# Weight conversion moved through a PSUM bank and spread over four head pairs of an attention stage; the last pair's running sums moved to VectorE

## The chip, the cores and the metric

The kernel runs on one core of one Trainium2 chip. The metric is the device time of one execution in microseconds, median of several runs. One execution of each kernel was also recorded by the hardware profiler, and all rows below come from that record.

## The reference

Three stages follow each other. Attention has 2 batches, 8 heads, 1152 keys and a head size of 64; neighbouring query rows are averaged, so that 576 queries remain for each head. Two MLPs (512 to 2048 to 512) then run over the 1152 tokens.

```python
q_pool = q.reshape(B, H, S // 2, 2, D).mean(axis=3)
scores = (1 / sqrt(D)) * q_pool @ k^T
attn = exp(scores - max(scores)) ; attn = attn / (sum(attn) + 1e-9)
x = (attn @ v) rearranged to [1152 tokens, 512]
x = leaky_relu(x @ moe_w_in, 0.01) @ moe_w_out
out = silu(x @ moe2_w_in) @ moe2_w_out
```

Query and key are scaled up in the inputs, so that the maximum has to be subtracted. Query, key and value are float32. The MLP weights are float64: the kernel sees each as a pair of 32-bit words and makes a float32 number of it (the "conversion" below), and each number is then split into a high part that TensorE reads directly and a low part.

## The kernel before

Attention takes the heads two at a time: eight pairs, p = 0 to 7. A pair has nine key tiles t and two heads j. These are its steps, with their lines:

- Transposes of queries and keys on TensorE (line 431), each held in a PSUM bank until ScalarE (line 348) and VectorE (lines 488, 527) have read it. These are done for the next pair while the present one runs.
- Maxima: 27 score tiles of the next pair are computed (lines 576 to 580) and each is reduced by VectorE straight out of its bank (line 584, tile `mx`). The row of maxima goes by small DMAs into the operand `ql` (line 602 onwards).
- Scores (line 634, tile `pss`), exponentials on ScalarE (line 638, tile `e`), and the product with the values (line 666, tile `pv`).
- Running sums over the key tiles, `acc += e` (line 655): 16 additions for a pair, t = 1 to 8 for each j. They run on GpSimd; in the last pair, seven of the 16 run on VectorE (`dve_last`).
- After a pair: the sums over the partitions (line 694, tile `psum`), a reciprocal that goes out and back by four DMAs with one VectorE instruction between them (line 729, tile `cmp`), and `finish` (lines 763 to 767): multiply, high part on ScalarE, low part on VectorE. The last pair has `sums_last` instead (lines 740 to 754), without DMAs.

The conversion of one piece of weights (128x512) has five steps in `convert_steps`: `begin` on ScalarE (line 127), then `clamp`, `shift`, `sign` and `tail` on VectorE (lines 131, 135, 139, 145). `clamp` and `shift` work in place on the tile `wt` in SBUF; `sign` and `tail` read one of the raw words (`wraw`, SBUF) and `wt`, and write `wt`. Eight pieces are converted during attention and 56 later, between the matmuls of the MLPs. Four of the eight are also split during attention (line 163 on ScalarE, line 167 on GpSimd).

The order of the instructions on each engine is made when the program is built, by a list scheduler (`Plan`). Every task has an engine, an assumed duration, a due time, and tokens that it takes and gives back. A task becomes ready when what it needs is done in the planner's own clock; among the ready tasks whose tokens are free, the one with the earliest due time comes next. The planner's clock gives a pair `t` = 30 us and the first begins at `t0` = 18 us. Its durations are guesses: they fix the order, and the engines then run it in order, each waiting where it must. Six PSUM banks (`bank`) are shared by transposes, maxima, scores and sums. TensorE runs in order too, and the first MLP's matmuls (line 923, tile `ph`) come behind the last pair's sums; the MLPs reuse attention's PSUM banks. A weight load takes one of three `raw` buffers, a conversion one of four `wt` buffers.

Of the kernel before, what the change touches and what calls it, by code (L numbers as in the profile page):

```python
# [8 lines left out]
F32 = mybir.dt.float32  # L9
F32R = mybir.dt.float32r  # L10
ACTF = mybir.ActivationFunctionType
ALU = mybir.AluOpType
U32 = mybir.dt.uint32
# [6 lines left out]
def pooled_attention_two_mlps(  # L20
# [28 lines left out]
    t=30.0,  # L49
# [5 lines left out]
    sums=1.15,  # L55
    norm=1.55,
    dve_add=(),
    dve_last=((3, 0), (4, 1), (5, 0), (6, 1), (7, 0), (8, 0), (8, 1)),
    low_pool=((0, 0, 1), (0, 1, 0), (0, 1, 1)),
    ql_pool=(0, 1),  # L60
    lead=3,
    load0=8.0,
    load1=12.0,
    weights=(-3.0, -0.3),
    conv=8,
    split=4,
    wt=4,
# [5 lines left out]
class Weights:  # L73
# [40 lines left out]
        for step in self.convert_steps():  # L114
            step()

    def convert_steps(self):
        nc = self.nc
        box = {}

        def begin():
            pairs = self.raw.pop(self.n_convert).rearrange("p (f w) -> p f w", w=2)
            box["low"], box["high"] = pairs[:, :, 0], pairs[:, :, 1]
            box["t"] = t = self.wt_p.tile(list(box["high"].shape), U32, tag="wt", name="wt")
            box["tf"] = self.mid[self.n_convert] = t.bitcast(F32)
            self.n_convert += 1
            nc.scalar.activation(out=box["tf"], in_=box["high"].bitcast(F32), func=ACTF.Abs, scale=65536.0)  # L127

        def clamp():
            tf = box["tf"]  # L130
            nc.vector.tensor_scalar(out=tf, in0=tf, scalar1=2.0, scalar2=W_TOP, op0=ALU.max, op1=ALU.min)  # L131

        def shift():
            t = box["t"]
            nc.vector.tensor_scalar(out=t, in0=t, scalar1=4, scalar2=1, op0=ALU.logical_shift_left, op1=ALU.logical_shift_right)  # L135

        def sign():
            t = box["t"]
            nc.vector.scalar_tensor_tensor(  # L139
                out=t, in0=box["high"], scalar=0x80000000, in1=t, op0=ALU.bitwise_and, op1=ALU.bitwise_or  # L140
            )

        def tail():
            t = box["t"]
            nc.vector.scalar_tensor_tensor(  # L145
                out=t, in0=box["low"], scalar=29, in1=t, op0=ALU.logical_shift_right, op1=ALU.bitwise_or
            )

        return begin, clamp, shift, sign, tail
# [35 lines left out]
class Plan:  # L185
# [15 lines left out]
    def add(self, engine, weight, due, emit=None, after=(), order=(), take=(), give=(), lag=None, begin=0.0):  # L201
        t = dict(
            engine=engine, weight=weight, due=due, emit=emit, take=take, give=give, left=0, at=begin, next=[],
            lag=self.LAG[engine] if lag is None else lag, n=len(self.tasks),
        )
        self.tasks.append(t)
        for x in after:
            self.edge(x, t)
        for x in order:
            self.edge(x, t, 0.0)  # L210
        return t
# [72 lines left out]
def attention(ctx, tc, q, k, v, xh, xl, weights):  # L284
# [8 lines left out]
    NP = B * H // 2  # L293
# [7 lines left out]
    P = PARAMS  # L301
    T0, T = P["t0"], P["t"]
# [11 lines left out]
    add = plan.add  # L314
    plan.tokens(bank=NBANK, qnat=1, knat=2, vnat=2, q2=1, ops=3, acc=2, pvs=1, v=1, r=1, raw=3, wt=P["wt"])
    plan.ring("e", NE)
    banks = list(range(NBANK))

    def bank(name):
        i = banks.pop(0)  # L320
        return ps_b.tile([128, 512], F32, tag=f"b{i}", name=name), i
# [16 lines left out]
    knat, qnat, vnat, q2, K2, QH, mx, acc, e_t, vps, pvs, rec, box = ({} for _ in range(13))  # L338
# [309 lines left out]
    def sum_up(p, t, j, after, order, due):  # L648
        on_dve = (p, t, j) in dve_adds

        def go():
            e = nc.vector if on_dve else nc.gpsimd
            if t == 1:
                acc[p, j] = sm_p.tile([128, SQ], F32, tag="acc", name="acc", bufs=4)
            e.tensor_tensor(out=acc[p, j], in0=e_t[p, j, 0] if t == 1 else acc[p, j], in1=e_t[p, j, t], op=ALU.add)  # L655

        take = ("acc",) if t == 1 and j == 0 else ()
        return add("DVE" if on_dve else "POOL", 1.2 if on_dve else 1.45, due, go, after=after, order=order, take=take)

    def pv(p, t, due, after, order):  # L660
        def go():
# [96 lines left out]
    def finish(p, after, due):  # L758
        b, hp = divmod(p, HP)
        cs = slice(b * SQ, (b + 1) * SQ)  # L760
        flat = lambda: pvs[p].rearrange("p a c -> p (a c)")
        x = add(
            "DVE", 0.95, due, lambda: nc.vector.tensor_tensor(out=pvs[p], in0=pvs[p], in1=rec.pop(p), op=ALU.mult),
            after=after, give=("r",),
        )
        x = add("ACT", 0.69, due, lambda: nc.scalar.activation(out=xh[:, hp, cs], in_=flat(), func=ACTF.Copy), after=[x])
        low = lambda: nc.vector.tensor_tensor(out=xl[:, hp, cs], in0=flat(), in1=xh[:, hp, cs], op=ALU.subtract)
        return add("DVE", 0.8, due + 1.0, low, after=[x], give=("pvs",))
# [24 lines left out]
    for p in range(NP):  # L793
        at = lambda x: T0 + (p + x) * T
        out = {}
        due = 0.0 if p == 0 else P["load1"] if p == 1 else at(P["load"])
# [23 lines left out]
        for n in range(NM):  # L820
            lo, hi = P["max"]
            due = 1.0 + 0.55 * n if p == 0 else at(lo + (hi - lo) * n / NM)
            j, u = n // NA, n % NA // NCH
            maxima.setdefault((j, u), []).append(max_tile(p, n, out, due))
        for j in range(2):
            after = scored.get((p - 3, j), []) + (filled[p] if p < 3 else [])
# [4 lines left out]
        steps = [(t, j) for t in range(NKT) for j in range(2)]  # L831
        if p == 0:
            steps = [(t, 0) for t in range(P["lead"])]
            for t in range(NKT):
                steps += [(t, 1)] + [(t + P["lead"], 0)] * (t + P["lead"] < NKT)
        for i, (t, j) in enumerate(steps):
            due = at(i / (2 * NKT))
# [5 lines left out]
        last = []  # L843
# [8 lines left out]
        values = evac_pv(p, last[0], at(1.0) + 1.0)  # L852
        ends = [av[NKT - 1, 0], av[NKT - 1, 1]]
        if p < NP - 1:
            finish(p, sums(p, ends, at(P["sums"])) + values, at(P["norm"]))
        else:
            finish(p, sums_last(p, ends, at(1.0)) + values, at(1.0))

    def weight_steps():
        convs, order = [], []
        n = P["conv"] + 3
        for i in range(n):
            lo, hi = P["weights"]
            begin = T0 + (NP + lo + (hi - lo) * i / n) * T
            due = T0 + (NP - 0.9 + 0.9 * i / n) * T
            x = add("SP", 0.5, due, weights.load, order=order, take=("raw",), lag=5.0, begin=begin)
            order = [x]
            if i >= P["conv"]:  # L870
                continue
            weigh = (("ACT", 0.66), ("DVE", 0.8), ("DVE", 1.0), ("DVE", 0.8), ("DVE", 0.8))
            for m, (step, (eng, w)) in enumerate(zip(weights.convert_steps(), weigh)):
                x = add(
                    eng, w, due, step, after=[x], order=convs[-1:] if m == 0 else [],
                    take=("wt",) if m == 0 else (), give=("raw",) if m == 4 else (),
                )
            convs.append(x)
        last = []
        for i in range(P["split"]):  # L880
            due = T0 + (NP - 1 + i / P["split"]) * T
            high, low = weights.split_steps()
            x = add("ACT", 0.62, due, high, after=[convs[i]], order=last)
            last = [add("POOL", 1.45, due, low, after=[x], give=("wt",))]

    weight_steps()
    plan.run()
# [186 lines left out]
```

## Time and profile before

| | |
|---|---|
| median of three runs (lowest, highest) | 687.91 us (686.66, 688.94) |
| the profiled execution | 688.05 us, its span 686.3 us |
| TensorE busy | 657.7 us, 96% of the span |
| VectorE, ScalarE, GpSimd busy | 466.6, 321.7, 398.9 us |
| mean granted TensorE clock | 0.985 of full speed |
| first matmul of the MLPs | at 274.32 us of the span |

The span runs from the first to the last instruction, and the execution's own time is 1.75 us longer. A stretch named below by its ends in microseconds counts from the start of the span. Engines are named in the rows as PE (TensorE), DVE (VectorE), ACT (ScalarE), POOL (GpSimd) and SP (SyncE, whose queue issues all DMAs). An instruction of one group may begin a little before the one ahead of it has ended, so sums of durations can be slightly above the busy time.

### The profile page before, as it was taken

The numbers are of one execution on the slowest core, as the hardware profiler recorded it, in microseconds if no ns is written. First come the engines' busy times: TensorE is split into PE (matmuls) and PEld (weight loads), VectorE is DVE, ScalarE is ACT, GpSimd is POOL, SyncE is SP. The second block draws the span as 40 slices with busy tenths as digits, with TensorE's granted clock in tenths as the row PEclk, the third lists the DMA queues.
The fourth block names the chain that finished last, engine by engine and source line by source line (L and its number), as shares of the span: only waits on it lengthen the run. The fifth ranks groups of instructions, "written<-read, shape, count | busy, mean of one in ns | idle before, by whom it ended". The sixth has DMA issues, their size and how long they took to land.

```text
span 686.3 us, 10321 instructions
## 1 busy us (share of the span) xinstructions
PE 657.7 (96%) x3741; PEld 533.7 (78%) x3741; DVE 466.6 (68%) x689; ACT 321.7 (47%) x694; POOL 398.9 (58%) x303
## 2 busy tenths in 40 slices
PE   6899999999979988999999999999989999999997
PEld 4566776767756754898988989999878898898986
DVE  6775758577789979497667567367666578877222
ACT  5446667575737555464533334244434543334120
POOL 7476888878868984565454354364634444455220
PEclk9899999999999999999999999999989999999999
DMA  5535151534634123032322223113122322220012
GB/s 147 154 79 140 36 139 37 156 80 125 182 84 120 49 63 105 5 124 93 123 92 78 77 94 91 62 60 95 61 77 78 92 93 69 88 89 1 0 47 92
DMA packets 41898, 59.71 MB, mean 87 GB/s; under 512 B 15324, under 2 KB 24568, under 8 KB 41848
## 3 DMA queue, kind: packets, MB, share of 16 engines
q1 hardware_dynamic: 41848, 59.07, 29.6%
q8 instruction: 29, 0.48, 0.3%
q14 instruction: 21, 0.17, 0.1%
HBM read 49.81 MB, written 2.42 MB: 76 GB/s over the span
## 4 chain that ended last, share of the span: by engine, by line
PE 76%; DVE 13%; issue 4%; ACT 4%; DMA 2%; SPq 1%; ACTq 0%; DVEq 0%
PE ph L923 25%; PE po L957 13%; PE pf L985 12%; PE pss L634 9%; PE pv L666 9%; PE pmx L580 4%; DVE mx L584 3%; PE prep L431 2%; DVE wt L135 2%; DVE wt L139 2%; DVE wt L131 2%; DVE a L942 1%; ACT wt L127 1%; DVE ql L488 1%; DVE wt L145 1%
## 5 line engine op out<-in xcount | busy, mean ns | idle before, releaser
L944 POOL TENSOR_TENSOR gl<-a,gh 128x512 fp32r<-128x512 f32 (+1 forms) x64 | 95.1, 1488 | 163.4 <-ACT gh L943 107.5
L655 POOL TENSOR_TENSOR acc<-acc,e 128x576 f32<-128x576 f32 x105 | 154.7, 1494 | 33.2 <-ACT e L638 27.4
L638 ACT ACTIVATE e<-pss 128x288 f32<-128x288 f32 x288 | 101.8, 411 | 84.9 <-PE pss L634 80.7
L584 DVE TENSOR_REDUCE mx<-pmx 128x1 f32<-128x384 f32 x216 | 110.5, 550 | 33.7 <-PE pmx L580 29.1
L923 PE MATMUL ph<-xh,w0h 128*128 128x320 f32 (+1 forms) x384 | 109.7, 340 | 4.2 <-DVE a L942 3.6
L923 PE MATMUL ph<-xl,w0h 128*128 128x320 f32 (+1 forms) x384 | 109.3, 339 | 0.0
L923 PE MATMUL ph<-xh,w0l 128*128 128x320 f32 (+1 forms) x384 | 109.0, 338 | 0.0
L131 DVE TENSOR_SCALAR wt<-wt 128x512 f32<-128x512 f32 x64 | 51.0, 797 | 81.4 <-ACT wt L127 72.6
L634 PE MATMUL pss<-qh,k 128*128 128x288 f32 x288 | 87.8, 321 | 2.2 <-DVE mx L584 2.0
L666 PE MATMUL pv<-e,vnat 128*64 128x288 f32 x576 | 87.7, 425 | 1.2 <-ACT e L638 1.2
L634 PE MATMUL pss<-ql,ka 128*128 128x288 f32 x288 | 82.2, 301 | 4.3 <-DMA ql<-mn 4.3
L923 PEld LDWEIGHTS ph<-xh,w0h 128*128 128x128 f32 x384 | 68.4, 191 | 12.0 <-DVE a L942 4.7
L923 PEld LDWEIGHTS ph<-xh,w0l 128*128 128x128 f32 x384 | 67.7, 190 | 5.0
L923 PEld LDWEIGHTS ph<-xl,w0h 128*128 128x128 f32 x384 | 67.9, 191 | 4.7
L634 PEld LDWEIGHTS pss<-qh,k 128*128 128x128 f32 x288 | 55.4, 192 | 20.2 <-issue 8.3
L580 PE MATMUL pmx<-k,qh 128*128 128x384 f32 x192 | 66.0, 383 | 4.9 <-DVE mx L584 3.0
L943 ACT ACTIVATE gh<-a 128x512 fp32r<-128x512 f32 (+1 forms) x32 | 22.0, 687 | 95.1 <-DVE a L942 95.1
L145 DVE SCALAR_TENSOR_TENSOR wt<-wraw,wt 128x512 uint32<-128x512 uint32 x64 | 62.6, 978 | 2.0
L135 DVE TENSOR_SCALAR wt<-wt 128x512 uint32<-128x512 uint32 x64 | 62.0, 970 | 2.1
L139 DVE SCALAR_TENSOR_TENSOR wt<-wraw,wt 128x512 uint32<-128x512 uint32 x64 | 58.7, 917 | 2.0
L666 PEld LDWEIGHTS pv<-e,vnat 128*64 128x64 f32 x576 | 35.6, 138 | 31.3 <-issue 14.3
L634 PEld LDWEIGHTS pss<-ql,ka 128*128 128x128 f32 x288 | 55.6, 193 | 5.0 <-DMA ql<-mn 3.0
(76 smaller groups left out, 1126.5 us busy)
## 6 DMA issues: line engine op xcount, KB each, us to landing
wraw<-in_moe_w_in_dram SPq DMA_DIRECT2D x32, 512.0 KB, 3.8
wraw<-in_moe_w_out_dram SPq DMA_DIRECT2D x32, 512.0 KB, 3.3
vnat<-in_v_dram SPq DMA_DIRECT2D x8, 576.0 KB, 4.8
qnat<-in_q_dram SPq DMA_DIRECT2D x16, 256.0 KB, 6.2
knat<-in_k_dram SPq DMA_DIRECT2D x7, 576.0 KB, 4.2
ka<-k SPq DMA_DIRECT2D x16, 160.0 KB, 2.6
out_dram<-acc SPq DMA_DIRECT2D x9, 256.0 KB, 2.0
ka<-k SPq DMA_DIRECT2D x16, 128.0 KB, 2.6
```

The source lines that it names most:

```text
L135: nc.vector.tensor_scalar(out=t, in0=t, scalar1=4, scalar2=1, op0=ALU.logical_shift_left, op1=ALU.logical_shift_right)
L139: nc.vector.scalar_tensor_tensor(out=t, in0=box["high"], scalar=0x80000000, in1=t, op0=ALU.bitwise_and, op1=ALU.bitwise_or)
L580: nc.tensor.matmul(out=ps[:, 0:KC], lhsT=QH[p, j][:, t * 128:(t + 1) * 128], rhs=K2[p, j][:, ks], start=True, stop=True)
L584: nc.vector.tensor_reduce(out=mx[p][:, n:n + 1], in_=ps[:, 0:KC], op=ALU.max, axis=AX.X)
L634: nc.tensor.matmul(out=ps[:, 0:C], lhsT=lhsT[:, ks], rhs=rhs[:, cs], start=not last, stop=last)
L638: nc.scalar.activation(out=e_t[p, j, t][:, cs], in_=ps[:, 0:C], func=ACTF.Exp, scale=scale)
L655: e.tensor_tensor(out=acc[p, j], in0=e_t[p, j, 0] if t == 1 else acc[p, j], in1=e_t[p, j, t], op=ALU.add)
L666: nc.tensor.matmul(out=vps[p, c][own[j], 0:C], lhsT=vnat[p][:, j, t, :], rhs=e_t[p, j, t][:, c * C:(c + 1) * C], start=(t == 0), stop=(t = ...
L923: nc.tensor.matmul(out=ps[:, c, 0:n], lhsT=wt[:, kk, fs], rhs=m[:, kk, chunk(g, c)], start=(kk == 0 and wt is wh and m is xh), stop=(kk == ...
L944: nc.gpsimd.tensor_tensor(out=gl[:, 0:nch * n], in0=a, in1=gh[:, 0:nch * n], op=ALU.subtract)
L957: nc.tensor.matmul(out=ps[:, c, 0:n], lhsT=wt[:, f, ms], rhs=x[:, c * n:(c + 1) * n], start=(f == 0 and wt is oh and x is gh), stop=(f == ...
L985: nc.tensor.matmul(out=ps[:, 0, :], lhsT=x[:, ts], rhs=wt[:, f, :], start=(f == 0 and x is gh and wt is oh), stop=(f == FB - 1 and x is gl),)
```

## The change

Four things differ. First, `convert_steps` takes an optional function `psum`; during attention it hands out one of the six shared banks. `begin` then writes the bank, `clamp`, `shift` and `sign` work in the bank, and only `tail` writes the SBUF tile `wt`; `sign` and `tail` have one operand in SBUF (`wraw`) and one in PSUM. The bank is taken at `begin` and given back after `tail`. The MLPs' own conversions call it without `psum` and stay as they were. Second, loads of weights may begin four pairs before the end of attention instead of three, and each is due one pair's time (30 us of the planner) after it may begin, instead of in the last pair; the splits come straight behind their conversion. Third, all 16 running sums of the last pair go to VectorE, instead of seven. Fourth, the planner's guesses change (conversion steps 0.6, 0.6, 0.7, 0.7 instead of 0.8, 1.0, 0.8, 0.8; a VectorE sum 0.85 instead of 1.2), and `finish` of the pair before the last is due 0.3 pairs later.

```diff
-    dve_last=((3, 0), (4, 1), (5, 0), (6, 1), (7, 0), (8, 0), (8, 1)),
+    dve_last=tuple((t, j) for t in range(1, 9) for j in range(2)),
...
-    weights=(-3.0, -0.3),
+    weights=(-4.0, -0.3),
+    weights_due=1.0,
...
-    def convert_steps(self):
+    def convert_steps(self, psum=None):
...
-            box["t"] = t = self.wt_p.tile(list(box["high"].shape), U32, tag="wt", name="wt")
-            box["tf"] = self.mid[self.n_convert] = t.bitcast(F32)
+            t = self.wt_p.tile(list(box["high"].shape), U32, tag="wt", name="wt")
+            box["out"], self.mid[self.n_convert] = t, t.bitcast(F32)
+            box["tf"] = psum() if psum else t.bitcast(F32)
+            box["t"] = box["tf"].bitcast(U32)
...
         def tail():
-            t = box["t"]
             nc.vector.scalar_tensor_tensor(
-                out=t, in0=box["low"], scalar=29, in1=t, op0=ALU.logical_shift_right, op1=ALU.bitwise_or
+                out=box["out"], in0=box["low"], scalar=29, in1=box["t"], op0=ALU.logical_shift_right, op1=ALU.bitwise_or
             )
...
-        return add("DVE" if on_dve else "POOL", 1.2 if on_dve else 1.45, due, go, after=after, order=order, take=take)
+        return add("DVE" if on_dve else "POOL", 0.85 if on_dve else 1.45, due, go, after=after, order=order, take=take)
...
-            finish(p, sums(p, ends, at(P["sums"])) + values, at(P["norm"]))
+            finish(p, sums(p, ends, at(P["sums"])) + values, at(P["norm"] + 0.3 * (p == NP - 2)))
...
-            due = T0 + (NP - 0.9 + 0.9 * i / n) * T
+            due = begin + P["weights_due"] * T
...
-            weigh = (("ACT", 0.66), ("DVE", 0.8), ("DVE", 1.0), ("DVE", 0.8), ("DVE", 0.8))
-            for m, (step, (eng, w)) in enumerate(zip(weights.convert_steps(), weigh)):
+            def psum(i=i):
+                box["conv", i] = bank("conv")
+                return box["conv", i][0]
+
+            steps = weights.convert_steps(psum)
+            weigh = (("ACT", 0.66), ("DVE", 0.6), ("DVE", 0.6), ("DVE", 0.7), ("DVE", 0.7))
+            for m, (step, (eng, w)) in enumerate(zip(steps, weigh)):
+                def go(step=step, m=m, i=i):
+                    step()
+                    if m == 4:
+                        banks.append(box.pop(("conv", i))[1])
+
                 x = add(
-                    eng, w, due, step, after=[x], order=convs[-1:] if m == 0 else [],
-                    take=("wt",) if m == 0 else (), give=("raw",) if m == 4 else (),
+                    eng, w, due, go, after=[x], order=convs[-1:] if m == 0 else [],
+                    take=("wt", "bank") if m == 0 else (), give=("raw", "bank") if m == 4 else (),
                 )
...
-        for i in range(P["split"]):
-            due = T0 + (NP - 1 + i / P["split"]) * T
-            high, low = weights.split_steps()
-            x = add("ACT", 0.62, due, high, after=[convs[i]], order=last)
-            last = [add("POOL", 1.45, due, low, after=[x], give=("wt",))]
+            if i < P["split"]:
+                high, low = weights.split_steps()
+                x = add("ACT", 0.62, due, high, after=[x], order=last)
+                last = [add("POOL", 1.45, due, low, after=[x], give=("wt",))]
```

## Rows read from the trace of the kernel before

**Rows 1.** The page: busy time by engine; the chain by engine:

```profile
...
PE 657.7 (96%) x3741; PEld 533.7 (78%) x3741; DVE 466.6 (68%) x689; ACT 321.7 (47%) x694; POOL 398.9 (58%) x303
...
PE 76%; DVE 13%; issue 4%; ACT 4%; DMA 2%; SPq 1%; ACTq 0%; DVEq 0%
...
```

**Rows 2.** Stretches, start:end and length; busy of five engines, TensorE clock, DMA:

```profile
...
121.70:151.40 29.70, 29.64 (x198) 20.65 (x197) 20.67 (x42) 18.98 (x51) 24.91 (x19) 1.00 0.40 99
151.40:180.90 29.50, 29.43 (x198) 20.64 (x197) 21.55 (x44) 19.60 (x52) 24.66 (x19) 1.00 0.48 125
180.90:216.50 35.60, 31.91 (x198) 21.79 (x197) 30.34 (x51) 20.67 (x54) 27.88 (x21) 0.95 0.48 131
216.50:247.70 31.20, 27.58 (x178) 18.78 (x177) 29.61 (x39) 17.31 (x46) 28.87 (x19) 0.98 0.28 82
247.70:274.30 26.60, 23.77 (x149) 14.11 (x148) 21.53 (x23) 15.29 (x41) 14.30 (x9) 0.95 0.29 86
...
```

**Rows 3.** Timeline of TensorE: start, length, instruction, idle before and its releaser:

```profile
...
191.97 0.40 PE L634 MATMUL pss<-qh,k 128*128 128x288 f32 x1 [1.01 <-DVE mx L584]
...
197.52 0.44 PE L580 MATMUL pmx<-k,qh 128*128 128x384 f32 x1 [2.53 <-DVE mx L584]
...
216.53 0.69 PE L694 MATMUL psum<-acc,ones 128*32 128x288 f32 x8
...
246.23 0.37 PE L634 MATMUL pss<-ql,ka 128*128 128x288 f32 x1 [2.83 <-DMA ql<-mn]
...
247.74 1.19 PE L694 MATMUL psum<-acc,ones 128*32 128x288 f32 x8
...
250.11 1.19 PE L666 MATMUL pv<-e,vnat 128*64 128x288 f32 x8
...
264.36 1.19 PE L666 MATMUL pv<-e,vnat 128*64 128x288 f32 x8
...
269.65 1.19 PE L666 MATMUL pv<-e,vnat 128*64 128x288 f32 x6 [1.24 <-ACT e L638]
...
272.55 1.19 PE L740 MATMUL psum<-acc,ones 128*64 128x288 f32 x6 [0.57 <-DVE acc L655]
274.32 0.50 PE L923 MATMUL ph<-xh,w0h 128*128 128x512 f32 x1 [0.59 <-ACT r L748]
...
285.34 0.45 PE L923 MATMUL ph<-xh,w0h 128*128 128x320 f32 x2
...
```

**Rows 4.** VectorE's groups, 178 to 274 us: count, busy, mean ns, idle before:

```profile
...
L135 DVE TENSOR_SCALAR wt<-wt 128x512 uint32<-128x512 uint32 x8 | 10.9, 1361 | 0.1
L145 DVE SCALAR_TENSOR_TENSOR wt<-wraw,wt 128x512 uint32<-128x512 uint32 x8 | 10.4, 1301 | 0.1
L139 DVE SCALAR_TENSOR_TENSOR wt<-wraw,wt 128x512 uint32<-128x512 uint32 x8 | 10.4, 1299 | 0.1
...
L131 DVE TENSOR_SCALAR wt<-wt 128x512 f32<-128x512 f32 x8 | 6.4, 805 | 3.9 <-ACT wt L127 3.8
...
```

**Rows 5.** Timeline of VectorE:

```profile
...
192.76 4.24 DVE L135 TENSOR_SCALAR wt<-wt 128x512 uint32<-128x512 uint32 x1
...
279.19 0.76 DVE L767 TENSOR_TENSOR xl<-pvs,xh 128x576 fp32r<-128x576 f32 x1 [0.81 <-ACT xh L766]
...
```

**Rows 6.** Instructions of lines 655 and 131, ns min/median/max:

```profile
...
L655 DVE TENSOR_TENSOR acc<-acc,e x7: 745/748/1978, 256.4 to 271.7; 128x576 f32<-128x576 f32 x7
...
L131 DVE TENSOR_SCALAR wt<-wt x64: 358/817/1869, 179.5 to 626.8; 128x512 f32<-128x512 f32 x64
...
```

**Rows 7.** Timeline of SyncE's DMA queue:

```profile
...
169.49 0.58 SPq L106 DMA_DIRECT2D wraw<-in_moe_w_in_dram  x1
...
```

**Rows 8.** VectorE's groups, 300 us to the end:

```profile
...
L971 DVE TENSOR_TENSOR acc<-po,acc 128x512 f32<-128x512 f32 x12 | 8.3, 688 | 16.8 <-PE po L957 16.8
```

**Rows 9.** VectorE's groups, 92.3 to 151.4 us (two stretches):

```profile
...
L488 DVE TENSOR_TENSOR ql<-prep,qh 64x512 fp32r<-64x512 f32 x4 | 2.8, 689 | 1.1 <-ACT qh L348 1.0
...
L729 DVE RECIPROCAL cmp<-cmp 128x9 f32<-128x9 f32 x2 | 0.4, 216 | 2.5 <-DMA cmp<-d 2.5
...
```

More of the change, by code (lines that the diff above doesn't have):

```diff
@@ L861, in weight_steps @@
     def weight_steps():
-        convs, order = [], []
+        convs, order, last = [], [], []
         n = P["conv"] + 3
@@ L871, in weight_steps @@
                 continue
-            weigh = (("ACT", 0.66), ("DVE", 0.8), ("DVE", 1.0), ("DVE", 0.8), ("DVE", 0.8))
-            for m, (step, (eng, w)) in enumerate(zip(weights.convert_steps(), weigh)):
+            def psum(i=i):
[8 more added lines that the diff above has]
+                        banks.append(box.pop(("conv", i))[1])
                 x = add(
-                    eng, w, due, step, after=[x], order=convs[-1:] if m == 0 else [],
-                    take=("wt",) if m == 0 else (), give=("raw",) if m == 4 else (),
+                    eng, w, due, go, after=[x], order=convs[-1:] if m == 0 else [],
+                    take=("wt", "bank") if m == 0 else (), give=("raw", "bank") if m == 4 else (),
                 )
             convs.append(x)
-        last = []
-        for i in range(P["split"]):
-            due = T0 + (NP - 1 + i / P["split"]) * T
-            high, low = weights.split_steps()
-            x = add("ACT", 0.62, due, high, after=[convs[i]], order=last)
-            last = [add("POOL", 1.45, due, low, after=[x], give=("wt",))]
+            if i < P["split"]:
+                high, low = weights.split_steps()
+                x = add("ACT", 0.62, due, high, after=[x], order=last)
+                last = [add("POOL", 1.45, due, low, after=[x], give=("wt",))]
     weight_steps()
```

## The prediction

> **What bounds the kernel now.** I read the page first. TensorE is busy for 96% of the span and holds 76% of the chain that ended last; VectorE holds 13% of it [rows 1]. So TensorE sets the time on the whole, and what is left to win lies where VectorE holds it up. The view of busy time by stretch says where that is. I cut it at the `psum` matmuls, which come once in a pair. Two ordinary stretches last 29.7 and 29.5 us, and TensorE is busy for all but 0.1 us of them. The next three last 35.6, 31.2 and 26.6 us with TensorE busy for 31.91, 27.58 and 23.77 us, at a mean granted clock of 0.95, 0.98 and 0.95 [rows 2]. These are the stretches in which the weights are converted.
>
> The timeline of TensorE then shows the waits: 1.01 and 2.53 us for VectorE's maxima, 2.83 us for the DMA of the row of maxima, 1.24 us for an exponential, and 0.57 us for the last running sum. The MLPs begin at 274.32 us [rows 3]. After that point the change touches nothing, so I sum up to it and carry the rest over unchanged.
>
> Why VectorE is late is read from its groups. The eight conversions take 6.4 + 10.9 + 10.4 + 10.4 = 38.1 us, 4.8 us each [rows 4]. One `shift` took 4.24 us, and TensorE's wait of 2.53 us ended as it did [rows 3, 5]. The same instruction can be short: `clamp` takes from 358 to 1869 ns, and a running sum on VectorE from 745 to 1978 ns [rows 6]. GpSimd is busy for 27.88 of 35.6 and 28.87 of 31.2 us of these stretches [rows 2], and all of these operands lie in SBUF.
>
> **The change part by part: what TensorE could win at most.** Stretch 180.9 to 216.5 has 198 matmuls, as an ordinary one has [rows 2]. It should take 29.5 us, which is 6.1 less. Stretch 216.5 to 247.7 has 178, since no pair follows whose operands need transposing. Its 27.58 us at a mean clock of 0.98 make 27.0 at 1.00; with 0.2 for joins it should take 27.2, which is 4.0 less. In the last stretch a key tile takes (264.36 - 250.11) / 6 = 2.375 us. From `psum` to the MLPs there would be 0.69 for `psum`, half of a tile's scores or (2.375 - 1.19) / 2 = 0.59, seven tiles or 16.6, the last two value products of 1.19, the last sums, which are as many matmuls as a value product and so 1.19, and the 0.59 for which ScalarE reads them [rows 3]: 22.0 us against 274.32 - 247.74 = 26.6, which is 4.6 less. Together 14.7 us.
>
> **Cost of a conversion.** `sign` and `tail` get one operand in PSUM and one in SBUF. The nearest rows are line 971 in the MLPs (PSUM and SBUF in, SBUF out, the same 128x512), with 688 ns [rows 8], and line 488 during attention, with 689 ns beside GpSimd's sums [rows 9]. I take 0.69 us for each. `clamp` and `shift` inside a bank are shown nowhere: below, they keep the shortest SBUF time, 0.36 us [rows 6]; above, 0.69 us. I take the upper end, as the rows with a PSUM operand are the nearer ones. A conversion is then 4 x 0.69 = 2.76 us and eight are 22 us, 16 less than now. ScalarE's `begin` has the same size as before (0.66 us by the planner), and its write to a bank is taken at no difference. ScalarE is idle for 10.7 of 29.7 us [rows 2]; were the write half as long again, that idle time would hide three times 0.33 us in a stretch, and without it eight would cost 2.6 us.
>
> The rule that speaks against the change is in the Trainium skill, "VectorE: DVE Perf Modes", section "Why PSUM operands drop a tier": a float32 operand in PSUM holds VectorE to one result a cycle, where two are possible in SBUF. By the rule the time is the 676.5 us worked out below; without it sixteen steps would take 0.33 us less each, the overrun of 2.1 us below would be gone, and the time would be 674.4 us.
>
> **Where the conversions lie.** The first load is now issued at 169.49 us [rows 7]. It may begin one pair, 30 us of the planner, earlier, so near 139.5, and the others follow by 3.7 x 30 / 11 = 10.1 us. With some 5 us to land, the conversions are spread from 145 to 216 us: one in stretch 121.7 to 151.4, three in each of the next two, the last after them. VectorE is busy for 21 us of an ordinary stretch [rows 2]; with three conversions it is 29.3. It also waits for the reciprocal's DMA, 2.5 us in two stretches, or 1.25 each [rows 9]. That is 30.5 against TensorE's 29.5, so each of the two full stretches runs 1.05 us over. After 210 us there is room: there VectorE has the same maxima, no transposes to read, and one or two conversions. The first conversion's stretch has 20.67 + 2.8 of 29.7 us and pays nothing.
>
> **The bank.** A conversion holds one of six banks from `begin` to `tail`. Queued behind `tail` on VectorE are maxima, and TensorE waits for these and for a free bank. No row prices five banks. Below it is nothing: TensorE hardly waits in ordinary stretches. Above, it is what one stretch loses today, 6.1 us. I take one wait like the 1.01 us of [rows 3] in all, since the planner counts the bank and places other work first.
>
> **The running sums.** Nine sums leave GpSimd and make 16 x 0.75 = 12 us on VectorE [rows 6]. With `finish` of the pair before (1.5 us) and one straggling conversion (2.8) that is 16.3 of 22.0 us. The last sum must end before TensorE is through with two value products, 2.38 us after the last scores; two exponentials at the planner's 0.42 and a sum take 0.84 + 0.75. So it lies hidden by 0.8 us; were it late, 0.57 us of wait stays. GpSimd has nothing left to do there, so the sums should run at their short time. `finish` due later lets exponentials pass ahead of it on ScalarE, which takes away the 1.24 us (counted in the 4.6).
>
> **SyncE's queue.** The same eleven loads are issued, two or three of them now among the key and query loads of an earlier pair. A late reciprocal behind them is part of the 1.25 us; a worse one is in the range.
>
> **Sum.** 14.7 - 2 x 1.05 - 1.0 = 11.6 us. Against the profiled execution's 688.05 us (0.14 above the median shown) this is 676.5 us (676.45).
>
> **Rivals.** *Contention stays in half of the steps.* `sign` and `tail` still read SBUF, and `tail` writes it. If they keep 1.30 us each [rows 4], a conversion costs 2 x 0.69 + 2 x 1.30 = 3.98 us. Each full stretch then needs 21 + 11.9 + 1.25 = 34.2 us, 4.7 over. That leaves 14.7 - 9.4 - 1.0 = 4.3 us: 683.8. So the part of the change that does what it says would be the running sums and half of the steps. Against it: line 971 also reads and writes SBUF, and its twelve of this size have a mean of 688 ns [rows 8]. The Trainium skill, "SBUF — State Buffer", section "Who interferes with whom", says that an instruction with at most one SBUF input does not contend with GpSimd, and the mean of 688 ns agrees.
>
> *`finish` becomes late.* The last pair's low part is ready at 279.95 us, and the MLPs need it at 285.34, a margin of 5.4 us [rows 3, 5]. `finish` of the pair before moves by 0.3 x 30 = 9 us, and the last pair's copy out waits for its one `pvs` buffer. If all 9 us come through, TensorE waits 3.6 us in the MLPs: 676.5 + 3.6 = 680.1. For it: there is a single buffer. Against it: a due time is an order among ready tasks, not a start.
>
> *Slower: the held bank.* With VectorE full in stretches 2 to 4 of the conversions, `tail` is late, a bank is missing, TensorE's queue stops at the next maximum, and its granted clock falls after the pause as it does now (0.95). The price is today's excess, 6.1 us, now in each of three stretches: 18.3 - 14.7 = 3.6 us more, 691.7. It decides for slower from (14.7 + 2.1) / 3 = 5.6 us for a stretch. Against it: such an excess took a 4.24 us `shift` [rows 5].
>
> *Same.* Bank and VectorE take some 4.6 us of each of three stretches, by the same mechanism: 14.7 - 13.8 = 0.9 us less, 687.1 us.
>
> **Chances.** The forecast (673 to 679.5 us) has 0.54. Contention has 0.18 and a late `finish` 0.08, together 679.5 to 686. Below 673, with VectorE's overrun and the bank costing nothing, 0.04. The same (within 0.3%, or 2.1 us, about what a measurement here can tell from no change) has 0.07, slower 0.09. Faster is thus 0.84. The range of 672 to 685 leaves out slower, same, and the ends of the other cases, about 0.2.
>
> **What the profile would show.** Right: `clamp` and `shift` near 0.69 us with little spread (0.4 would be a gift), `sign` and `tail` at 0.69; `psum` of pairs 4 to 6 near 182, 212.5 and 240 us; the MLPs' first matmul near 262.7; 16 sums on VectorE at 0.75 us; and a granted clock near 1.00 in these stretches. Wrong: steps above 1 us beside GpSimd (contention); TensorE waiting for maxima or for line 145 in stretches from 150 us on (bank); a wait of the second `ph` group for `xl` (`finish`). The MLPs should take 412 us as before; if they don't, my carrying over is wrong.

## The result and the profile after

The changed kernel takes 680.89 us (median of four runs, 679.80 to 681.43) against 688.2 for the kernel before; the ratio is 0.9893, with a 95% interval of 0.9879 to 0.9908. Its profiled execution took 679.80 us with a span of 678.0, against 688.05 and 686.3. It became faster by 7.3 us in the medians and 8.25 in the profiled executions; 11.6 were forecast, so it lies 4.4 us above the forecast of 676.5, inside the range of 672 to 685 and above the narrower 673 to 679.5.

The view of busy time by stretch, for the changed kernel, cut at the same `psum` matmuls as in [rows 2] (start:end, length, TensorE, weight loads, VectorE, ScalarE, GpSimd, clock, DMA); the last row is the MLPs:

```profile
...
152.18:185.19 33.01, 30.45 (x198) 20.58 (x198) 25.70 (x52) 21.43 (x56) 27.22 (x22) 1.00 0.58 150
185.19:216.43 31.24, 30.33 (x198) 20.40 (x198) 26.58 (x52) 20.56 (x54) 26.46 (x21) 1.00 0.51 143
216.43:244.24 27.81, 27.61 (x181) 18.45 (x180) 21.45 (x41) 16.22 (x44) 22.82 (x16) 1.00 0.32 91
244.24:265.92 21.68, 21.09 (x147) 13.39 (x146) 13.47 (x20) 13.14 (x38) 0.00 (x0) 1.00 0.15 41
265.92:678.00 412.08, 402.09 (x2160) 358.94 (x2160) 256.72 (x311) 158.90 (x271) 187.30 (x132) 0.99 0.23 74
...
```

The stretches that [rows 2] gave as 29.5, 35.6, 31.2 and 26.6 us now last 33.0, 31.2, 27.8 and 21.7. So the first, an ordinary one before, has become slower, and the other three give back 4.4, 3.4 and 4.9 us. About two thirds of that is time in which TensorE stood still (3.7, 3.6 and 2.8 us before, 0.9, 0.2 and 0.6 now); the rest lies in its busy time. The first `psum` of all came 0.8 us later than before (63.56 against 62.80 us); its place varied between 61.9 and 63.7 us in the kernels below, so I count it as scatter. The MLPs take 412.08 us against 411.98. TensorE's mean granted clock is 1.00 in all four stretches; before, three of them had 0.95, 0.98 and 0.95.

VectorE's groups from 135 to 270 us (line numbers are a few higher than before: 135, 139, 143 and 148 are `clamp`, `shift`, `sign` and `tail`; 658 is the running sum, 587 the maximum):

```profile
...
L658 DVE TENSOR_TENSOR acc<-acc,e 128x576 f32<-128x576 f32 x14 | 10.2, 755 | 5.7 <-ACT e L641 5.7
...
L139 DVE TENSOR_SCALAR conv<-conv 128x512 uint32<-128x512 uint32 x8 | 5.5, 692 | 0.1
L143 DVE SCALAR_TENSOR_TENSOR conv<-wraw,conv 128x512 uint32<-128x512 uint32 x8 | 5.5, 691 | 0.1
L135 DVE TENSOR_SCALAR conv<-conv 128x512 f32<-128x512 f32 x8 | 5.5, 691 | 1.4 <-ACT conv L131 1.4
L148 DVE SCALAR_TENSOR_TENSOR wt<-wraw,conv 128x512 uint32<-128x512 uint32 x8 | 5.5, 683 | 0.3
...
```

Every step of a conversion takes 0.69 us, as was priced. Eight conversions cost 5.5 x 4 = 22.0 us where they cost 38.1 [rows 4]. The running sums on VectorE take 0.755 us. What was priced wrong is what stays between TensorE's own pace and the stretches. TensorE's timeline in the first full stretch:

```profile
...
162.76 0.40 PE L637 MATMUL pss<-qh,k 128*128 128x288 f32 x1 [0.81 <-DVE mx L587]
...
165.02 0.40 PE L637 MATMUL pss<-qh,k 128*128 128x288 f32 x1 [0.64 <-DVE mx L587]
...
185.19 0.69 PE L697 MATMUL psum<-acc,ones 128*32 128x288 f32 x8 [0.74 <-DVE mx L587]
...
```

A score matmul or the sums' matmul needs nothing from a maximum except its PSUM bank, so these waits for line 587 are waits for a bank. [rows 3] had them too (1.01 us), but only in the stretches of the conversions. VectorE in the same stretch, and last one step of a conversion in the MLPs, still in SBUF, for comparison:

```profile
...
162.08 0.22 DVE L732 RECIPROCAL cmp<-cmp 128x9 f32<-128x9 f32 x1 [2.44 <-DMA cmp<-d]
...
163.08 0.69 DVE L135 TENSOR_SCALAR conv<-conv 128x512 f32<-128x512 f32 x1
163.81 0.70 DVE L139 TENSOR_SCALAR conv<-conv 128x512 uint32<-128x512 uint32 x1
...
184.49 0.56 DVE L587 TENSOR_REDUCE mx<-pmx 128x1 f32<-128x384 f32 x1 [0.51 <-PE pmx L583]
...
283.60 0.42 DVE L135 TENSOR_SCALAR wt<-wt 128x512 f32<-128x512 f32 x1
...
```

VectorE stood for 2.44 us before the reciprocal, whose small DMA had not landed, with maxima queued behind it; two conversion steps then went between the maxima that TensorE waited for. These are the pauses of 0.81 and 0.64 us. The third, 0.74 us, is of another kind: VectorE itself was idle for 0.51 us until TensorE's last score tile, and TensorE waited for that tile's maximum to free a bank for the sums. A conversion lay in one of the six banks from 182.2 to 187.1 us.

### The profile page after: what moved, and what is told of

Read it like the earlier page. It is cut to its first block, busy times and chain, and to the rows that moved or that the text cites. A ratio compares the mean times of both kernels' runs of the same rounds, so it can differ in the third digit from the quotient of the medians.

```text
span 678.0 us, 10325 instructions
## 1 busy us (share of the span) xinstructions
PE 654.2 (97%) x3741; PEld 530.3 (78%) x3741; DVE 452.3 (67%) x698; ACT 320.7 (47%) x694; POOL 379.6 (56%) x294
## 4 chain that ended last, share of the span: by engine, by line
PE 77%; DVE 12%; ACT 4%; DMA 3%; issue 2%; POOL 0%; SPq 0%; ACTq 0%; DVEq 0%
PE ph L934 24%; PE po L968 13%; PE pf L996 12%; PE pss L637 10%; PE pv L669 10%; PE pmx L583 4%; DVE mx L587 3%; PE prep L434 2%; DVE wt L139 2%; DVE wt L135 2%; DVE wt L143 1%; DMA d<-sum 1%; DVE a L953 1%; ACT wt L131 1%; DVE ql L491 1%
## 5 line engine op out<-in xcount | busy, mean ns | idle before, releaser
L658 POOL TENSOR_TENSOR acc<-acc,e 128x576 f32<-128x576 f32 x98 | 140.1, 1451 | 29.0 <-ACT e L641 26.6
L135 DVE TENSOR_SCALAR wt<-wt 128x512 f32<-128x512 f32 x56 | 44.6, 796 | 77.3 <-ACT wt L131 68.6
L170 POOL TENSOR_TENSOR w1l<-wt,w1h 128x512 fp32r<-128x512 f32 x32 | 44.0, 1381 | 39.8 <-ACT w1h L166 39.8
L996 PE MATMUL pf<-w1h,gh 128*128 128x512 f32 x144 | 56.5, 392 | 0.4 <-DVE a L953 0.3
L996 PE MATMUL pf<-w1h,gl 128*128 128x512 f32 x144 | 56.2, 390 | 0.6 <-POOL gl L955 0.6
```

The costliest lines, as they stand in the source:

```text
L170: self.nc.gpsimd.tensor_tensor(out=lo, in0=tf, in1=hi, op=ALU.subtract)
L996: nc.tensor.matmul(out=ps[:, 0, :], lhsT=x[:, ts], rhs=wt[:, f, :], start=(f == 0 and x is gh and wt is oh), stop=(f == FB - 1 and x is gl),)
```

## The experiments

Three parts of the change were tried alone or undone (bank, sums, spreading), and seven kernels asked what the remaining overrun is. All ratios are to the kernel before on the same chip; the changed kernel stands at 0.9893 (0.9879 to 0.9908).

| kernel | median, us | ratio (95%) |
|---|---|---|
| bank alone | 679.13 | 0.9868 (0.9848 to 0.9888) |
| sums alone | 694.04 | 1.0081 (1.0049 to 1.0114) |
| changed, bank undone | 690.08 | 1.0034 (1.0021 to 1.0048) |
| changed, over seven pairs | 685.94 | 0.9975 (0.9957 to 0.9994) |
| changed, spreading undone | 679.30 | 0.9885 (0.9841 to 0.9929) |
| changed, sums undone | 680.54 | 0.9896 (0.9869 to 0.9923) |
| changed, reciprocal later | 682.21 | 0.9919 (0.9899 to 0.9940) |
| bank alone, reciprocal later | 680.11 | 0.9887 (0.9861 to 0.9912) |
| changed, thin steps | 681.31 | 0.9895 (0.9856 to 0.9933) |
| before, five banks | 690.83 | 1.0048 (1.0027 to 1.0068) |
| changed, prompt steps | 699.40 | 1.0158 (1.0130 to 1.0186) |
| bank alone, later conversions | 678.77 | 0.9871 (0.9849 to 0.9894) |

**The bank alone.** Only the first part of the change; loads, due times and sums as before.

```diff
-    dve_last=tuple((t, j) for t in range(1, 9) for j in range(2)),
+    dve_last=((3, 0), (4, 1), (5, 0), (6, 1), (7, 0), (8, 0), (8, 1)),
...
-    weights=(-4.0, -0.3),
-    weights_due=1.0,
+    weights=(-3.0, -0.3),
...
```

> The kernel before with only the conversion moved into a PSUM bank (and the planner's four guesses for its steps); times of loads, splits and the last pair's running sums as before. Theory A (the price of a conversion is what counts): the eight conversions fall from 38.1 to 22 us of VectorE, the stretches between the sums of pairs 4 and 6 (66.8 us before) fall by 7 to 9 us, the last stretch (26.6) by 1 to 2, and the time to 678 to 681 us. Rival B (it is the spreading that counts, the bank alone does little): 685 to 688 us, and the conversions still end in the last stretch.

Measured: 679.13 us. Its stretches:

```profile
...
180.03:216.85 36.82, 33.02 (x198) 21.31 (x197) 28.40 (x55) 22.32 (x58) 28.37 (x22) 0.95 0.52 147
216.85:244.45 27.60, 27.58 (x181) 18.48 (x180) 22.96 (x43) 16.79 (x45) 23.86 (x17) 1.00 0.35 104
244.45:266.00 21.55, 20.96 (x148) 13.45 (x147) 12.49 (x15) 13.67 (x39) 13.29 (x9) 1.00 0.21 65
...
```

The bank by itself gives all of the gain, and the time is theory A's. Its stretches are not: the two from the sums of pair 4 on fall by 2.4 us instead of 7 to 9, and the last by 5.0 instead of 1 to 2, so that the total came out right partly by luck. The last stretch is at TensorE's own pace, 21.55 us, with nine sums still on GpSimd (13.29 us of its time) and one conversion in it. One stretch in this execution is poor: 36.8 us, with a mean clock of 0.95 and a wait of 4.02 us before the reciprocal. VectorE's and TensorE's row there:

```profile
...
191.42 0.21 DVE L731 RECIPROCAL cmp<-cmp 128x9 f32<-128x9 f32 x1 [4.02 <-DMA cmp<-d]
...
```

```profile
...
192.10 0.40 PE L636 MATMUL pss<-qh,k 128*128 128x288 f32 x1 [2.30 <-DVE mx L586]
...
```

TensorE stood for 2.30 us until the first maximum behind the reciprocal was done; from 194 to 198 us its granted clock was 0.59 and 0.56.

**The sums alone.**

```diff
-    dve_last=((3, 0), (4, 1), (5, 0), (6, 1), (7, 0), (8, 0), (8, 1)),
+    dve_last=tuple((t, j) for t in range(1, 9) for j in range(2)),
...
-        return add("DVE" if on_dve else "POOL", 1.2 if on_dve else 1.45, ...)
+        return add("DVE" if on_dve else "POOL", 0.85 if on_dve else 1.45, ...)
...
-            finish(p, ..., at(P["norm"]))
+            finish(p, ..., at(P["norm"] + 0.3 * (p == NP - 2)))
```

> The kernel before with only the running sums of the last pair moved to VectorE (the guess for one, and the later finish of the pair before, go with it); conversions in SBUF at their old times. Theory A: GpSimd is idle in the last stretch, sums and conversions there run at their short times, the stretch falls from 26.6 to 22 to 23.5 us, nothing else moves, 684 to 685 us. Rival: VectorE then has twelve microseconds of sums and three conversions in one stretch and is late, 687 to 690 us.

Measured: 694.04 us, slower than expected by either theory. Its last stretch, one row of VectorE's timeline in it, and TensorE's last sums:

```profile
...
248.47:278.16 29.69, 24.84 (x150) 14.79 (x149) 19.62 (x32) 15.16 (x41) 0.00 (x0) 0.84 0.25 82
...
```

```profile
...
269.52 0.43 DVE L131 TENSOR_SCALAR wt<-wt 128x512 f32<-128x512 f32 x1 [2.56 <-ACT wt L127]
...
```

```profile
...
274.72 2.85 PE L740 MATMUL psum<-acc,ones 128*64 128x288 f32 x8 [4.26 <-DVE acc L655]
...
```

It was not a lack of time: VectorE is busy for 19.62 of 29.69 us, and the sums run at 0.75 us. The last conversion's first step waits 2.56 us for ScalarE, three sums are queued behind it in VectorE's order, and TensorE waits 4.26 us for them. Its granted clock is 0.84 in this stretch, and 0.50 from 274 to 282 us, after this wait: the MLPs start on it and take 414.6 us instead of 412.0.

**The changed kernel with the bank undone.** Spreading and sums stay; conversions work in SBUF again.

```diff
-            steps = weights.convert_steps(psum)
-            weigh = (("ACT", 0.66), ("DVE", 0.6), ("DVE", 0.6), ("DVE", 0.7), ("DVE", 0.7))
+            steps = weights.convert_steps()
+            weigh = (("ACT", 0.66), ("DVE", 0.8), ("DVE", 1.0), ("DVE", 0.8), ("DVE", 0.8))
...
```

> The changed kernel with the bank alone undone: conversions in SBUF again (with the planner's old guesses), spread over four pairs, all sums of the last pair on VectorE. Theory A: a conversion costs 4 to 5 us again wherever GpSimd adds, so the stretches from pair 3 to pair 6 need 7 to 10 us more than in the changed kernel and it ends at 686 to 691 us. Rival B (spreading and sums do it): 680 to 683 us, as the changed kernel.

Measured: 690.08 us, as theory A had it. VectorE's groups from 135 to 276 us:

```profile
...
L143 DVE SCALAR_TENSOR_TENSOR wt<-wraw,wt 128x512 uint32<-128x512 uint32 x8 | 14.0, 1756 | 0.1
L139 DVE TENSOR_SCALAR wt<-wt 128x512 uint32<-128x512 uint32 x8 | 12.1, 1518 | 0.2
L148 DVE SCALAR_TENSOR_TENSOR wt<-wraw,wt 128x512 uint32<-128x512 uint32 x8 | 11.1, 1387 | 0.1
...
L135 DVE TENSOR_SCALAR wt<-wt 128x512 f32<-128x512 f32 x8 | 6.2, 776 | 0.1
...
```

The same 32 instructions on the same amount of data take 43.4 us in SBUF and 22.0 through the bank; `sign` and `tail` fall from 1.76 and 1.39 us to 0.69, although both still read and one writes SBUF. Without the bank the conversions are dearer than before (43.4 against 38.1); a likely reason, not tested, is that spreading puts more of them into stretches where GpSimd adds.

**Over seven pairs.** One constant: `weights=(-7.0, -0.3)`.

> The changed kernel with the loads and conversions spread over seven pairs instead of four (from -7.0 instead of -4.0). The three stretches after 152 us lasted 92.1 us in the changed kernel and 86.2 would be bare. Theory A (the overrun comes from how much is squeezed into a stretch): with half as many conversions in each the overrun falls from 5.9 to 2 to 3 us in all, 677 to 679 us. Rival C (each conversion costs a fixed wait, through the bank it holds, wherever it lies): the sum of overruns stays at 5 to 6 us, only over more stretches, 680 to 682 us.

Measured: 685.94 us. Both theories had it no slower than 682. Its five stretches before the one without transposes last 29.3, 33.8, 31.1, 32.1 and 33.4 us. Two of them:

```profile
...
92.91:126.74 33.83, 30.50 (x198) 20.67 (x197) 27.05 (x51) 21.20 (x57) 27.29 (x22) 1.00 0.44 124
...
189.92:223.29 33.37, 30.96 (x199) 21.90 (x198) 23.24 (x47) 19.33 (x52) 24.61 (x19) 0.95 0.47 114
...
```

VectorE is busy for only 27.1 and 23.2 us of these. The overruns add up to 12.1 us against 5.2 in the changed kernel's two full stretches: they grew as more stretches held a conversion, not with how full VectorE was. But the waits before the reciprocal grew too, to 3.36 us in the fourth of the five stretches and 4.22 in the fifth (the second row shown), where TensorE then stood for 1.20 and 2.40 us; in the second stretch (the first row) its longest pause was 1.64 us, for an exponential. So the kernel does not separate the two.

**Spreading undone, sums undone.** The changed kernel with the loads, due times and splits of before (first), and the changed kernel with the sums of before (second).

> The bank and the sums on VectorE, with loads, conversions and splits at their old times: the changed kernel without the spreading. Theory: in the kernel with only the bank the last stretch is already 21.6 us with nine sums on GpSimd, at TensorE's own pace, so moving the sums wins nothing: 678.5 to 680.5 us. Rival (conversions and sums together hold up the last stretch, as with the sums alone, where it lasted 29.7): 682 to 687 us.

> The bank and the spreading, with nine of the 16 sums of the last pair on GpSimd as before: the changed kernel without the moved sums. Theory: the last stretch stays at 21.5 to 22.5 us and the time at that of the changed kernel, 680 to 682 us. Rival (GpSimd and VectorE in turns at the sums cost what they cost before): the last stretch is 23 to 26 us, 682 to 685 us.

Measured: 679.30 and 680.54 us. Two stretches of the first, and the last stretch of the second:

```profile
...
179.94:213.84 33.90, 31.48 (x198) 20.63 (x197) 28.43 (x55) 22.25 (x58) 28.47 (x22) 1.00 0.57 160
...
241.45:262.89 21.44, 20.84 (x147) 13.13 (x146) 15.82 (x24) 13.66 (x39) 0.00 (x0) 1.00 0.21 66
...
```

```profile
...
246.58:268.13 21.55, 20.96 (x148) 13.45 (x147) 9.69 (x11) 13.15 (x38) 13.28 (x9) 1.00 0.14 41
...
```

With the bank, moving the sums changes nothing that can be measured, in either order of conversions: the last stretch is 21.4 to 21.7 us with or without it. Spreading moves the overrun (33.9 us in one stretch instead of 33.0 and 31.2 in two) and wins nothing that can be measured.

**The reciprocal later.** Two guesses raised, in the changed kernel and in the kernel with the bank alone.

```diff
-        x = dma(due, down, after=[x])
-        x = dma(due, up, after=[x])
+        x = dma(due, down, after=[x], lag=4.8)
+        x = dma(due, up, after=[x], lag=2.8)
```

> The changed kernel with two guesses of the planner raised: 4.8 us instead of 2.2 for the DMA of the sums out, 2.8 instead of 2.2 for the one that brings them back, so that the reciprocal (the instruction behind these DMAs) is put later in VectorE's order. Nothing else is changed. Theory D (the overrun comes from VectorE standing still before the reciprocal, 2.4 and 1.3 us in the two full stretches, with maxima queued behind it and one bank less): the waits for the DMA fall below 0.5 us, the stretches of 33.0 and 31.2 us fall to 30 to 30.7, 677 to 678.5 us. Rival C (each conversion costs a wait through its bank): the waits for the DMA go, the stretches stay at 31 to 33, 680 to 682 us.

> The kernel with only the bank, and the same two guesses raised. Its stretch of 36.8 us holds a wait of 4.0 us before the reciprocal and ran at a mean granted clock of 0.95. Theory D: that stretch falls to 30 to 31.5 us at a clock of 1.00, 673 to 675 us. Rival C: 677 to 680 us.

Measured: 682.21 and 680.11 us; both forecasts of theory D fell. The first full stretch of the changed kernel with this edit, two rows of VectorE's timeline in it and one of TensorE's:

```profile
...
153.85:186.80 32.95, 30.91 (x198) 20.67 (x197) 28.09 (x53) 21.04 (x56) 27.25 (x21) 1.00 0.51 144
...
```

```profile
...
165.09 0.21 DVE L732 RECIPROCAL cmp<-cmp 128x9 f32<-128x9 f32 x1
...
174.06 1.32 DVE L766 TENSOR_TENSOR pvs<-pvs,r 128x576 f32<-128x576 f32 x1 [0.94 <-DMA r<-d]
...
```

```profile
...
176.44 0.44 PE L583 MATMUL pmx<-k,qh 128*128 128x384 f32 x1 [1.02 <-ACT e L641]
...
```

The wait before the reciprocal is gone, and the stretch is as long as ever. What is computed from the reciprocal is now late, line 766 waits 0.94 us for the next DMA of that chain, and TensorE paused for 1.02 us at 176.44 us for a bank that an exponential had not yet emptied. The edit holds for every pair and lengthened other stretches too (the last from 21.7 to 22.6 us). In the other kernel a wait of 2.59 us before the reciprocal remained. So the wait was moved and not taken away, and this pair of kernels can't say what it costs.

**Thin steps.** `clamp`, `shift` and `sign` work on two of 512 columns.

```diff
+        def cols():
+            return 2 if psum else box["tf"].shape[1]
...
-            tf = box["tf"]
+            tf = box["tf"][:, 0:cols()]
...
```

> The changed kernel with clamp, shift and sign of the eight conversions during attention working on two columns of 512 (so those weights are not converted: work is left out). The order of every engine's instructions and the holding of the bank from begin to tail stay; about 8 x 3 x 0.6 = 14 us of VectorE's work go. Theory E (the overrun of the two full stretches, 33.0 and 31.2 us against 29.5, is VectorE's time: maxima wait behind conversion steps): both fall to 29.5 to 30.3 us, 676 to 678 us. Rival C (it is the bank: TensorE has five banks while a conversion lies in the sixth, some 80 us in all): they stay at 30.8 to 33 us, 679.5 to 681 us.

Measured: 681.31 us. Two of VectorE's groups, and the two full stretches:

```profile
...
L142 DVE TENSOR_SCALAR conv<-conv 128x2 uint32<-128x2 uint32 x8 | 1.3, 161 | 0.1
...
L138 DVE TENSOR_SCALAR conv<-conv 128x2 f32<-128x2 f32 x8 | 1.3, 158 | 2.4 <-ACT conv L131 2.4
...
```

```profile
...
151.47:186.03 34.56, 32.34 (x198) 21.34 (x198) 24.25 (x52) 21.09 (x56) 26.80 (x22) 0.95 0.56 150
186.03:217.21 31.18, 30.15 (x197) 20.41 (x197) 23.73 (x51) 20.48 (x54) 26.85 (x21) 1.00 0.48 132
...
```

8 x 3 x 0.53 = 12.7 us of conversion work are gone over all stretches, and these two last 34.6 and 31.2 us. VectorE's busy time in them fell by only 1.45 and 2.85 us: other steps lie in the neighbouring stretches, and the multiply of `finish` became dearer (mean 1.45 us instead of 0.87 in the changed kernel). The second stretch is the clean comparison, 31.18 us against 31.24 with the clock at 1.00 in both; there theory E falls, and the overrun is not VectorE's busy time. The first had a granted clock of 0.50 from 174 to 176 us and 0.68 in the next two, after TensorE had been busy for only 1.18 and 1.52 us of the two steps of 2 us before, so its length says less. One pause did go with the work: the 0.64 us behind two conversion steps has no counterpart.

**Five banks.** `NBANK = 5` in the kernel before.

> The kernel before with five PSUM banks instead of six for the whole of attention, nothing else changed; the planner orders for five. Rival C: ordinary stretches, 29.4 to 29.7 us with six, become 31 to 33 us, and with six such stretches the time is 8 to 20 us longer, 696 to 708 us. Theory E: five banks are enough, ordinary stretches stay below 29.9 us, 687 to 690 us.

Measured: 690.83 us. Three stretches in which no weights are converted, and the matmul that starts the second, with VectorE's row before it:

```profile
...
63.09:93.52 30.43, 29.73 (x198) 20.60 (x198) 21.43 (x44) 19.01 (x51) 25.19 (x20) 1.00 0.37 97
93.52:125.64 32.12, 29.65 (x197) 20.61 (x198) 22.43 (x43) 18.81 (x50) 24.04 (x20) 1.00 0.38 95
125.64:156.12 30.48, 29.77 (x198) 20.63 (x199) 20.59 (x43) 18.80 (x50) 25.03 (x20) 1.00 0.42 101
...
```

```profile
...
93.52 0.69 PE L694 MATMUL psum<-acc,ones 128*32 128x288 f32 x8 [0.56 <-DVE mx L584]
...
```

```profile
...
92.81 1.02 DVE L584 TENSOR_REDUCE mx<-pmx 128x1 f32<-128x384 f32 x2 [1.42 <-PE pmx L580]
...
```

Ordinary stretches of 29.5, 29.4 and 29.7 us become 30.4, 32.1 and 30.5, or 1.5 us more on average (the next one 30.4, 0.9 more). A bank thus has a price, between the two theories' figures: less than rival C had it and more than nothing. The pause before the sums' matmul is the one that the changed kernel has at 185.19 us: VectorE is idle, and TensorE waits for a maximum to free a bank. It stands at four of the `psum` matmuls (0.56 or 0.57 us each), and at none in the kernel before.

**Prompt steps.** Once begun, a conversion's steps come first on VectorE.

```diff
-                    eng, w, due, go, after=[x], ...
+                    eng, w, due if m == 0 else 0.0, go, after=[x], ...
```

> The changed kernel with the four VectorE steps of a conversion due at once as soon as they are ready, so that they follow each other and the bank is held for 3.5 to 5 us instead of 3.7 to 18.6. VectorE's work is the same, and maxima wait for up to 2.8 us in a row. Rival C: the overruns halve, 676.5 to 678.5 us. Theory E: they stay or grow, since maxima now wait longer at a time, 680.5 to 684 us.

Measured: 699.40 us. One stretch lasted 47.8 us. A row of the chain of waits in it (start, length), and what VectorE waited for:

```profile
...
194.22 7.16 DMA cmp<-d
...
```

```profile
...
201.47 0.21 DVE L732 RECIPROCAL cmp<-cmp 128x9 f32<-128x9 f32 x1 [11.03 <-DMA cmp<-d]
...
```

The new order put the loads of the next pair and copies of keys ahead of the DMA that brings 4.5 KB of sums back. It took 7.16 us, VectorE stood for 11.03, and TensorE for 6.16. Neither theory had such a time. This kernel changed more than the bank's hold, so it says nothing about rival C.

**Later conversions.** The bank alone, with `weights=(-2.4, -0.3)`.

> The kernel with only the bank, with loads and conversions begun 0.6 pairs later (from -2.4 instead of -3.0), so that fewer conversions lie in the stretch from the sums of pair 4 to those of pair 5 and more in the next, which has no transposes. Theory F (a conversion costs TensorE time only in a stretch that also has the transposes of a next pair, where five banks and the order of VectorE leave no slack; the stretch without them lasted 27.6 us with four conversions against 27.2 bare): the first of these stretches falls from 33.9 to 36.8 us to 30 to 32, the next stays below 28.5, 673.5 to 677 us. Rival C (each conversion costs a fixed wait wherever it lies): 678.5 to 680.5 us. Rival G (the conversions come too late and hold the last stretch or the MLPs' weights): the last stretch is 23 us or more, 680 to 685 us.

Measured: 678.77 us, the same as the bank alone within the intervals. Its last three stretches, and TensorE's waits at the end:

```profile
...
181.13:211.15 30.02, 29.94 (x199) 20.67 (x198) 23.11 (x46) 19.40 (x53) 24.64 (x19) 1.00 0.58 155
211.15:240.54 29.39, 29.09 (x192) 19.41 (x191) 22.55 (x41) 18.99 (x52) 27.59 (x20) 1.00 0.33 97
240.54:264.79 24.25, 20.22 (x137) 12.26 (x135) 22.73 (x27) 14.24 (x38) 13.24 (x10) 1.00 0.27 89
...
```

```profile
...
260.70 0.70 PE L742 MATMUL psum<-acc,ones 128*64 128x288 f32 x2 [1.49 <-DVE acc L657]
262.63 1.18 PE L742 MATMUL psum<-acc,ones 128*64 128x288 f32 x6 [1.23 <-DVE acc L657]
...
```

The stretch with transposes falls to 30.0 us as theory F had it, but it holds four conversion steps instead of twelve, and VectorE waited for only 0.65 us before the reciprocal. The next two last 53.6 us together instead of 49.2, against theory F and in kind like rival G. The `psum` that parts them came later (192 and 137 matmuls instead of 181 and 148), and TensorE is idle for only 0.3 us of the first, so the loss lies in the last: there TensorE waits 1.49 and 1.23 us for running sums that share VectorE with late conversions. Of the 6.8 us won in one stretch, 4.5 were given back there. Sums wholly on VectorE together with these later conversions was not tried.

## Why the prediction was right in kind and too hopeful in size

- The time lies in the band that I had given to contention and to a late `finish` (679.5 to 686), and neither of them came. That it is inside the range is owed to the range's width; the mechanism was mine, with the overrun at nearly twice its price: TensorE waiting for maxima, which I had named as a sign of being wrong, came.
- *The price of a conversion* was right: 0.69 us for each step, 22 us for eight, beside a GpSimd that is busy for 27.2 of the 33.0 us. The Trainium skill, "VectorE: DVE Perf Modes", section "Why PSUM operands drop a tier", has a float32 operand in PSUM cap an instruction at the lowest of VectorE's rates. This trace agrees: `clamp` took 0.42 us in SBUF at 283.60 us and takes 0.69 in the bank. The loss on two steps is small beside what leaving SBUF saves.
- *Contention in half of the steps* did not come: `sign` and `tail` have one operand in SBUF and stay at 0.69 us. That is as the Trainium skill, "SBUF — State Buffer", section "Who interferes with whom", has it for instructions with at most one SBUF input outside the two-port modes, a condition that my prediction left out.
- *TensorE's own pace* was right where it could be reached: 27.2 us forecast against 27.6 to 27.8, and 22.0 against 21.4 to 21.7.
- *The overrun* is the term that was mis-sized, and the step that failed: 2 x 1.05 us for VectorE and 1.0 for the bank, 3.1 in all. Measured are 33.0 - 29.5 = 3.5, 31.2 - 29.5 = 1.7 and 27.8 - 27.2 = 0.6, so 5.8. These 2.7 us more, the 0.8 before the first `psum` and the 0.1 in the MLPs, less 0.3 in the last stretch, are the 3.3 by which the profiled execution fell short of the forecast.
- The sentence that failed is "That is 30.5 against TensorE's 29.5". It summed VectorE's work as if the engine were full, with three conversions in each stretch. There were eight and ten steps, or 2 and 2.5 conversions, in the two full stretches and three in the next; VectorE was busy for 25.7 of 33.0 and 26.6 of 31.2 us, and 2.85 us less of its work left the second as long as it was.
- *What the runs show in its place:* TensorE waits for banks. In the first full stretch it stands still for 2.56 us. Of these, 0.81 end with the first maximum behind the late reciprocal, 0.64 with a maximum behind two conversion steps, and 0.74 stand where the kernel with five banks has the like pause with VectorE idle; short waits make up the rest. The other 1.0 us of the 3.5 is busy time of TensorE (30.45 against 29.43 before), which no run takes apart. The price of a missing bank for a whole stretch was 0.8 to 2.7 us in the kernel with five, above the 1.0 in all that I took.
- *The late reciprocal* I had put into VectorE's sum at 1.25 us a stretch. In the traces of all fourteen kernels VectorE waited for it 14 times by 2.4 us or more, and each time TensorE paused (for 0.58 to 6.16 us) and went on 0.68 or 0.69 us after the reciprocal began, behind the first maximum. Waits of up to 1.91 us cost TensorE nothing, or 0.18 us once. So these pauses come from that wait; what would be won by taking it away is not shown, since the kernels that moved it got other waits. The shares for the second full stretch and the third (1.7 and 0.6 us) stay open too.
- *The sums on VectorE* lie hidden, as worked out, but I credited the last stretch's 4.6 us partly to them and to the later `finish`. The bank alone has the same last stretch. The sums alone are slower (0.0081 x 687.9 = 5.6 us). The late conversion that I had put into the last stretch was not there.
- *The spreading* was to make room on VectorE. With the bank it wins nothing that can be measured: it put the price of the bank and of the late reciprocal into a stretch that was undisturbed before. Over seven pairs it costs most of the gain.
- *`finish` late* did not come: the last pair's low part was ready at 271.55 us, 5.4 before its use, the same margin as before.

## What to carry to other kernels

When two engines hold each other up over SBUF, find out which operands can lie in PSUM: a step may look slower there and still halve what it costs in company. Test the parts of such a change singly: here one part gave everything, one did nothing beside it and harmed alone, and the spreading only moved the loss. And do not price a crowded stretch by an engine's summed busy time when engines run in order and share buffers; look for who waits for whose buffer, and for the small transfer that a busy engine waits for in order.

## What was not expected of the hardware

- A DMA of 4.5 KB took 1.67 us from issue to use in the changed kernel, 3.60 in the kernel with only the bank and 7.16 in the kernel with prompt steps; the one that takes the sums out, of the same size, took 4.7 to 5.4 us in the same chains.
- In the kernel before, the changed kernel and the kernel with only the bank, a weight load is issued shortly ahead of the sums in the first poor stretch (180.22, 154.82 and 179.33 us), and 5.1, 4.9 and 5.4 us pass from the issue of the DMA out to that of the DMA back, against 3.7 to 4.6 in the ordinary stretches before. With later conversions the first load comes behind the reciprocal (190.33 us), 4.0 us pass, and VectorE waits for 0.65. That the load is the cause was not tested by itself.
- The spread of VectorE's steps through the bank was nearly nothing (means of 683 to 692 ns for all four), where the same steps in SBUF had means of 776 to 1756 ns in one stretch of GpSimd's sums.
